# Where the halves of g lie in a partition: 0 and 192 bytes modulo 256, in place of 192 and 192

## The chip, the cores and the metric

The kernel runs on one NeuronCore of a Trainium2 chip. The metric is the device time of one execution in microseconds: 608.89 us, the median of 3 runs (608.73 to 609.63). The engines are named as in the profile: PE is TensorE's matmuls and PEld its weight loads, DVE is VectorE, ACT ScalarE, POOL GpSimd and SP SyncE, which issues the transfers.

## The reference

A windowed attention with block summaries, then a feed-forward layer with a squared ReLU:

```python
k_sum = k.reshape(B, H, nb, block, D).max(axis=3)
v_sum = v.reshape(B, H, nb, block, D).mean(axis=3)
scores_l = scale * q @ k.T          # masked to |i - j| < 16
scores_s = scale * q @ k_sum.T + np.log(block)
a = softmax(concatenate([scores_l, scores_s], -1))
x = a @ concatenate([v, v_sum], axis=2)      # heads put side by side: 3072 x 512
h = x @ w_in                                 # 512 x 2048
r = np.maximum(h, 0.0)
g = s * (r * r) + b
return g @ w_out                             # 2048 x 512
```

There are 4 batches of 768 rows, 8 heads of 64, blocks of 32 keys. All inputs are float32.

## The kernel before

The 3072 rows are worked in 12 chunks of 256 (three to a batch). For each chunk the attention of its four pairs of heads gives x in transposed form; then the hidden layer is made in 16 blocks f of 128 features, and each block is projected back onto 512 output columns.

The feed-forward products keep float32's accuracy by splitting each operand into an upper half, rounded to the matmul's number format, and a lower half, the remainder: xh and xl, wh and wl, gh and gl. A product is the sum of three matmuls, lower x upper, upper x lower, upper x upper. For the hidden layer (`hidden`, L460) the weights are the stationary operand, which a weight load brings into TensorE before the matmul, and x streams past them, 256 columns at a time: per block 4 matmuls of xh with wl, 4 of xl with wh, 4 of xh with wh. For the projection (`project`, L504; the last four blocks in `project_last`, L514) g is the stationary operand and w_out's half streams past it, 512 columns at a time: per block and per 128 rows one matmul with gl and wh, one with gh and wl, one with gh and wh. So gh is loaded twice and gl once.

Two blocks share one tile of g, 128 x 512. It is made by `activate` (ScalarE: ReLU out of the accumulators at L468, square at L474), `scaled` (GpSimd, L481), `upper_rows` (VectorE, a cast into gh, L219) and `lower_rows` (VectorE, r minus gh into gl, L492). r has two buffers, gh and gl four each.

The order of work on every engine is written out: a long list of names for the first chunks, then a table of steps. From the third chunk on TensorE alternates between runs of 48 hidden matmuls (4 blocks) and runs of 24 projection matmuls (4 blocks of the earlier ones), and once in a chunk does the attention's value products (L417) and scores (L301) for later chunks.

The sums of v over blocks, for batches 1 to 3, are made on the way. For each of two groups g of heads `v_sum` reduces three thirds of v (VectorE, L172) into the tile vhalf, and `v_mean` scales it (ScalarE, L178) into vmean, from which four transfers take it to vsum. vhalf has two buffers, so that the second group can be reduced while the first still waits for its scaling.

Tiles lie in a partition one after the other, in the order in which their pools first see them. What matters here, as addresses in bytes within a partition, before the change:

| tile | buffers | address of each | modulo 256 |
|---|---|---|---|
| wh (w_in and w_out upper) | 8 | 4352 to 61696, 8192 apart | 0 |
| wl | 17, in a ring | 69888 to 135424, 4096 apart | 0 |
| xh, xl | 2 and 2 | 171456, 175552; 179648, 183744 | 192 |
| r | 2 | 187840, 189888 | 192 |
| gh | 4 | 191936, 193984, 196032, 198080 | 192 |
| gl | 4 | 200128, 202176, 204224, 206272 | 192 |
| vhalf | 2 | 208320, 208576 | 192 |

The parts of these tiles that a matmul or a load reads begin at multiples of 512 bytes from the tile's start, so they lie at the same place modulo 256 as the tile.

Of the kernel before, what the change touches and what calls it, by code (L numbers as in the profile page):

```python
# [11 lines left out]
F32 = mybir.dt.float32  # L12
# [7 lines left out]
P = 128  # L20
B, H, S, D = 4, 8, 768, 64
# [8 lines left out]
T = NSUB * SUB  # L30
# [14 lines left out]
def windowed_attention_then_relu2_ffn(ctx, tc, qk, vwin, kt, vt, kq, vrow, wp, out):  # L45
# [8 lines left out]
    p2 = ctx.enter_context(tc.tile_pool(name="p2", bufs=2))  # L54
# [48 lines left out]
    w_raw, w_f, w_h, w_l, held = {}, {}, {}, {}, {}  # L103
# [43 lines left out]
    kraw, ksum, vraw, vhalf, vsum = {}, {}, {}, {}, {}  # L147
# [19 lines left out]

    def v_sum(bi, g, third):
        if third == 0:
            vhalf[bi, g] = p2.tile([96, D], F32, name="vhalf")  # L170
        dst = vhalf[bi, g][:, slice(*THIRDS[third])]
        nc.vector.tensor_reduce(dst, vraw.pop((bi, g, third))[:96], axis=AX.X, op=ALU.add)  # L172

# [55 lines left out]
    def place(c):  # L229
        return c // PER_B, c % PER_B  # L230
# [205 lines left out]
    ph_of, gg, po = {}, {}, {}  # L436
# [25 lines left out]
            )  # L462

    def activate(c, q, other=0):
        gg[c, q] = r = p2.tile([P, 2 * T], F32, name="r")
        ph = ph_of.pop((c, q))
        if other < 2:
            nc.scalar.activation(r, ph, AF.Relu)  # L468
        else:
            nc.vector.tensor_scalar(r, ph, 0.0, None, ALU.max)  # L470
        if other % 2:
            nc.vector.tensor_tensor(r, r, r, ALU.mult)
        else:
            nc.scalar.activation(r, r, AF.Square)  # L474
# [13 lines left out]

    def lower_rows(c, q):
        g, gh = gg[c, q]  # L490
        gl = p2.tile([P, 2 * T], F32R, name="gl", bufs=4)
        nc.vector.tensor_tensor(gl, g, gh.bitcast(F32), ALU.subtract)  # L492
        gg[c, q] = gh, gl
# [68 lines left out]
    def of(fn, *more):  # L562
# [9 lines left out]
        "Ai": of(scale_weights, "in"), "Ao": of(scale_weights, "out"), "A": of(scale_weights, "both"),  # L572
        "Bi": of(convert_weights, "in"), "Bo": of(convert_weights, "out"), "D": of(convert_weights, "both"),
        "Y": hidden_part, "H": hidden, "J": activate, "G": scaled, "a": upper_rows, "b": lower_rows,
        "P": project, "O": evict, "h": upper_weights, "l": lower_weights,
    }
# [20 lines left out]
    for c in range(2, NC):  # L597
        bi, ci = place(c)
        for p in range(NPAIR):
# [4 lines left out]
            if ci == 0:  # L604
                then(base - 12 + p, LOAD, load_k, bi, p)
                then(base - 7 + p, ATT, k_max, bi, p)
                if p < 2:
                    for third in range(3):
                        then(base + v_at - 5 + third, LOAD, load_v, bi, p, third)
                        then(base + v_at - 2 + third // 2, ATT, v_sum, bi, p, third)  # L610
                    then(base + v_at, ATT, v_mean, bi, p)
# [23 lines left out]
    for i in range(NF, NC * NF):  # L635
        c, f = divmod(i, NF)

        then(i - i % 4, HID, hidden, c, f)
        if f % 2:
            for stage_of in (activate, scaled, upper_rows, lower_rows):  # L640
                then(i, CHAIN, stage_of, c, f // 2)
        if i >= NC * NF - 4:
            if f == NF - 1:
                then((i + 4) | 3, PROJ, project_last)
            continue
        then((i + 4) | 3, PROJ, project, c, f)
        if f == NF - 1:
            for t in range(T // P):
                then((i + 4) | 3, EVICT, evict, c, t)
# [60 lines left out]
```

## Time and profile before

| what | before |
|---|---|
| median of 3 runs | 608.89 us |
| the profiled execution, its time | 609.05 us |
| the profiled execution, its span | 607.3 us |
| granted TensorE clock | 0.999 |
| PE busy | 598.1 us (98%) |
| DVE, ACT, POOL busy | 419.5, 275.9, 138.9 us |
| L504, three groups of 376 matmuls | 148.0, 147.7, 147.5 us |
| L460, three groups of 760 matmuls | 119.0, 117.8, 117.6 us |

The span runs from the first to the last instruction; the time has some 1.75 us more around it. Matmuls overlap in the trace, since each is shown from its start to the end of its pipeline: the pace is read from the distance between starts, not from their lengths. In the chain of waits, "in order of time", a row gives start, length and what, with a run of one line's matmuls put together; the length of such a run is free of that overlap.

### The profile page before, as it was taken

Reading aid. Unit: us, or ns where it says so; the run is one execution under the profiler, and the core shown is the slowest. Engines: PE = TensorE matmul, PEld = TensorE weight load, DVE = VectorE, ACT = ScalarE, POOL = GpSimd, SP = SyncE. Lnnn points to the kernel's source line nnn. Section 1 sums busy time; section 2 is a strip of 40 time slices with the busy share of each in tenths; the row PEclk is TensorE's granted clock in tenths of the full one; section 3 lists DMA queues with packets and bytes.
Section 4 is the critical chain, followed back from the end, with each engine's and each line's share of the span. In section 5 each row is a group of like instructions: output and inputs, shape, how many; then the busy total and the mean of one; then the engine's idle time right before and its main releaser. Section 6 shows DMA issues by size and latency. Waiting matters only on the chain.

```text
span 607.3 us, 13540 instructions
## 1 busy us (share of the span) xinstructions
PE 598.1 (98%) x5240; PEld 539.7 (89%) x5240; DVE 419.5 (69%) x1128; ACT 275.9 (45%) x712; POOL 138.9 (23%) x275
## 2 busy tenths in 40 slices
PE   7999999999999999999999999999999999999997
PEld 6798898899989998998999899999998998899896
DVE  6999988789589378668758648847858827832212
ACT  5999998261352262263163254235235235223221
POOL 5420012211511411412141411331151151141110
PEclk9999999999999999999999999999999999999999
DMA  8999723025405016103503211600630500200000
GB/s 337 389 386 389 270 84 113 1 72 156 137 3 186 1 46 225 58 20 107 169 20 100 88 45 64 220 18 20 176 101 1 187 9 12 87 2 1 36 2 35
DMA packets 27281, 66.41 MB, mean 109 GB/s; under 512 B 3856, under 2 KB 4368, under 8 KB 27216
## 3 DMA queue, kind: packets, MB, share of 16 engines
q1 hardware_dynamic: 27216, 65.55, 31.0%
q8 instruction: 41, 0.67, 0.5%
q14 instruction: 24, 0.20, 0.1%
HBM read 59.09 MB, written 6.29 MB: 108 GB/s over the span
## 4 chain that ended last, share of the span: by engine, by line
PE 94%; ACT 3%; DMA 1%; DVE 1%; issue 0%; SPq 0%; DVEq 0%
PE ph L460 43%; PE po L504 43%; PE pav L417 4%; PE ps L301 3%; ACT pr L336 1%; DMA wraw<-in_wp_dram 1%; PE po L514 1%; PE pt L379 0%; PE ph L441 0%; ACT wraw L122 0%; ACT wraw L123 0%; SPq L240 0%; ACT pT L221 0%; DVE pr L346 0%; ACT vsum L221 0%
## 5 line engine op out<-in xcount | busy, mean ns | idle before, releaser
L481 POOL TENSOR_SCALAR r<-r,sb_col 128x512 f32<-128x512 f32 x85 | 69.4, 817 | 392.6 <-ACT r L474 259.6
L468 ACT ACTIVATE r<-ph 128x512 f32<-128x512 f32 x93 | 55.4, 596 | 206.8 <-PE ph L460 172.6
L504 PE MATMUL po<-wh,gh 128*128 128x512 f32 x376 | 148.0, 393 | 0.0
L504 PE MATMUL po<-wh,gl 128*128 128x512 f32 x376 | 147.7, 393 | 0.0
L504 PE MATMUL po<-wl,gh 128*128 128x512 f32 x376 | 147.5, 392 | 0.0
L219 DVE CAST gh<-r 128x512 fp32r<-128x512 f32 x88 | 38.1, 433 | 131.7 <-POOL r L481 130.8
L368 DVE STREAM_TRANSPOSE pT<-pr 32x256 f32<-32x256 f32 x288 | 125.4, 436 | 4.1
L460 PE MATMUL ph<-xh,wl 128*128 128x256 f32 x760 | 119.0, 279 | 0.0
L460 PE MATMUL ph<-xl,wh 128*128 128x256 f32 x760 | 117.8, 277 | 0.0
L460 PE MATMUL ph<-xh,wh 128*128 128x256 f32 x760 | 117.6, 277 | 0.0
L460 PEld LDWEIGHTS ph<-xh,wl 128*128 128x128 f32 x760 | 104.8, 188 | 5.2 <-DVE wl L144 0.3
L460 PEld LDWEIGHTS ph<-xl,wh 128*128 128x128 f32 x760 | 101.3, 188 | 0.0
L460 PEld LDWEIGHTS ph<-xh,wh 128*128 128x128 f32 x760 | 100.7, 188 | 0.0
L504 PEld LDWEIGHTS po<-wh,gl 128*128 128x128 f32 x376 | 70.6, 188 | 15.0 <-issue 1.1
L504 PEld LDWEIGHTS po<-wh,gh 128*128 128x128 f32 x376 | 70.7, 188 | 14.4
L504 PEld LDWEIGHTS po<-wl,gh 128*128 128x128 f32 x376 | 70.6, 188 | 13.8
L336 ACT ACTIVATE pr<-pr,mn 128x120 f32<-128x120 f32 x176 | 67.0, 383 | 22.2 <-DVE mn L323 22.0
L492 DVE TENSOR_TENSOR gl<-r,gh 128x512 fp32r<-128x512 f32 x96 | 69.3, 722 | 4.1 <-ACT gh L221 1.3
L474 ACT ACTIVATE r<-r 128x512 f32<-128x512 f32 x92 | 58.2, 632 | 5.7 <-DVE r L470 2.9
L263 POOL COPY vw<-vsum 24x256 f32<-24x256 f32 x88 | 47.2, 574 | 26.5 <-DMA vsum<-vmean 13.2
L346 DVE TENSOR_TENSOR pr<-pr,rs 128x480 f32<-128x480 f32 x48 | 32.9, 685 | 2.4 <-ACT pr L336 0.5
L221 ACT COPY o<-po 128x512 f32<-128x512 f32 (+1 forms) x23 | 13.1, 570 | 46.3 <-PE po L504 36.0
(94 smaller groups left out, 495.3 us busy)
## 6 DMA issues: line engine op xcount, KB each, us to landing
wraw<-in_wp_dram SPq DMA_DIRECT2D x32, 512.0 KB, 8.3
qk<-in_qk_dram SPq DMA_DIRECT2D x44, 369.0 KB, 5.7
vw<-in_vwin_dram SPq DMA_DIRECT2D x48, 256.0 KB, 3.6
out_dram<-o SPq DMA_DIRECT2D x22, 256.0 KB, 2.0
kraw<-in_kt_dram SPq DMA_DIRECT2D x12, 384.0 KB, 5.5
vraw<-in_vt_dram SPq DMA_DIRECT2D x12, 252.0 KB, 3.1
kq<-in_kq_dram SPq DMA_DIRECT2D x4, 512.0 KB
vraw<-in_vt_dram SPq DMA_DIRECT2D x6, 264.0 KB, 3.2
```

The costliest lines, as they stand in the source:

```text
L219: nc.vector.tensor_copy(out_, in_)
L263: nc.gpsimd.tensor_copy(vw_t[c, p][WIN:KR, e], vsum[bi][WIN : WIN + NB, 2 * p + e, :].unsqueeze(1).to_broadcast([NB, NSUB, D]),)
L336: nc.scalar.activation(pr, pr, AF.Exp, bias=mn_of[c, p][:, n : n + 1], scale=-1.0, accum_out=sm_of[c, p][:, n : n + 1])
L346: nc.vector.tensor_tensor(pr, pr, rs.unsqueeze(2).to_broadcast([P, 4, KR]), ALU.mult)
L368: nc.vector.transpose(to[BLOCK * k : BLOCK * (k + 1), :, rows], src)
L417: nc.tensor.matmul(oi, vw[:KR, e, i, :], pi[:KR], start=True, stop=True)
L460: nc.tensor.matmul(ph, w[:, kc * P : (kc + 1) * P], x[:, kc], start=(n == 0), stop=(n == len(terms) - 1))
L468: nc.scalar.activation(r, ph, AF.Relu)
L474: nc.scalar.activation(r, r, AF.Square)
L481: (nc.vector if other else nc.gpsimd).tensor_scalar(g, g, s_col, b_col, ALU.mult, ALU.add)
L492: nc.vector.tensor_tensor(gl, g, gh.bitcast(F32), ALU.subtract)
L504: nc.tensor.matmul(po[c, t], a[:, t * P : (t + 1) * P], w[:, 512:], start=(f == 0 and n == 0), stop=(f == NF - 1 and n == len(terms) - 1),)
```

## The change

The upper halves gh are put at 0 bytes modulo 256; everything that lies behind gl stays where it was. The two buffers of r are made 32 bytes longer each, which moves gh by 64 bytes; a tile of 192 bytes, which nothing writes or reads, is placed between gh and gl; and vhalf, which lies behind gl, has one buffer in place of two, which gives the 256 bytes back.

```diff
     def v_sum(bi, g, third):
         if third == 0:
-            vhalf[bi, g] = p2.tile([96, D], F32, name="vhalf")
+            vhalf[bi, g] = p2.tile([96, D], F32, name="vhalf", bufs=1)
         dst = vhalf[bi, g][:, slice(*THIRDS[third])]
         nc.vector.tensor_reduce(dst, vraw.pop((bi, g, third))[:96], axis=AX.X, op=ALU.add)
...
     def activate(c, q, other=0):
-        gg[c, q] = r = p2.tile([P, 2 * T], F32, name="r")
+        gg[c, q] = r = p2.tile([P, 2 * T + 8], F32, name="r")[:, : 2 * T]
         ph = ph_of.pop((c, q))
...
     def lower_rows(c, q):
         g, gh = gg[c, q]
+        if ("gap", 0) not in held:
+            held["gap", 0] = p2.tile([P, 48], F32, name="gap", bufs=1)
         gl = p2.tile([P, 2 * T], F32R, name="gl", bufs=4)
```

| tile | address of each, changed kernel | modulo 256 |
|---|---|---|
| r | 187840, 189920 | 192, 224 |
| gh | 192000, 194048, 196096, 198144 | 0 |
| gl | 200384, 202432, 204480, 206528 | 192 |
| vhalf | 208576 | 192 |

All other tiles keep their addresses. The order of instructions is the same on every engine. One wait is added, three times (once for each of batches 1 to 3): on VectorE, at the first reduction of the second group of heads (`vhalf` is the tile of sums, `vraw` the raw v). Before:

```order
L172 TENSOR_REDUCE vhalf<-vraw 96x21 [waits DMAHW4_49]
L172 TENSOR_REDUCE vhalf<-vraw 96x22 [waits DMAHW2_49]
L172 TENSOR_REDUCE vhalf<-vraw 96x21 [waits DMAHW5_49]
L368 STREAM_TRANSPOSE pT<-pr 32x8x32 x4
L219 CAST gh<-r 128x512 [waits PE_49,Pool_49]
L492 TENSOR_TENSOR gl<-r,gh 128x512 [waits DVE_49]
```

The same place in the changed kernel, whose later line numbers are two higher:

```order
L172 TENSOR_REDUCE vhalf<-vraw 96x21 [waits DMAHW4_49]
L172 TENSOR_REDUCE vhalf<-vraw 96x22 [waits DMAHW2_49,Activation_49]
L172 TENSOR_REDUCE vhalf<-vraw 96x21 [waits DMAHW5_49]
L368 STREAM_TRANSPOSE pT<-pr 32x8x32 x4
L219 CAST gh<-r 128x512 [waits PE_49,Pool_49]
L494 TENSOR_TENSOR gl<-r,gh 128x512 [waits DVE_49]
```

The reduction of 22 columns, the first of the second group, now waits for ScalarE too: for the scaling of the first group's sums (L178), which reads the buffer that it is to overwrite.

## The prediction

> **What bounds the kernel now.** I read the page's busy shares and chain first, then the chain in order of time for the steady part, then the order of single matmuls there. First the page:
>
> ```profile
> span 607.3 us, 13540 instructions
> PE 598.1 (98%) x5240; PEld 539.7 (89%) x5240; DVE 419.5 (69%) x1128; ACT 275.9 (45%) x712; POOL 138.9 (23%) x275
> ...
> PEclk9999999999999999999999999999999999999999
> ...
> PE 94%; ACT 3%; DMA 1%; DVE 1%; issue 0%; SPq 0%; DVEq 0%
> ...
> L460 PE MATMUL ph<-xh,wl 128*128 128x256 f32 x760 | 119.0, 279 | 0.0
> ```
>
> TensorE is busy 98% of the span at a full granted clock and holds 94% of the chain. Nothing that another engine does can win much; what counts is the pace at which TensorE starts one matmul after the other. The chain in order of time (start, length, what) shows that pace for one chunk of 256 rows:
>
> ```profile
> 311.19 5.70 PE po L504 x24
> 316.89 5.47 PE ph L460 x48
> 322.36 5.49 PE po L504 x24
> 327.85 5.47 PE ph L460 x48
> 333.32 5.49 PE po L504 x24
> ...
> 355.24 2.02 PE pav L417 x64
> 357.25 1.80 PE ps L301 x64
> 359.05 5.70 PE po L504 x24
> ```
>
> A chunk takes 359.05 - 311.19 = 47.9 us, and all but the 2.02 and 1.80 of them, 44.0, are runs of hidden (L460) and project (L504). The same two runs look different earlier:
>
> ```profile
> 124.63 5.66 PE ph L460 x48
> 130.29 5.51 PE po L504 x24
> 135.80 5.66 PE ph L460 x48
> ...
> 158.14 5.65 PE ph L460 x48
> 163.79 2.02 PE pav L417 x64
> ...
> 173.31 5.47 PE ph L460 x48
> ```
>
> Here 48 matmuls of the same shape take 5.66 us, after the next attention stage 5.47 us. Inside a run, the single matmuls (start, length, instruction):
>
> ```profile
> 326.31 0.39 PE L504 MATMUL po<-wh,gl 128*128 128x512 f32 x1
> 326.54 0.39 PE L504 MATMUL po<-wl,gh 128*128 128x512 f32 x1
> 326.77 0.39 PE L504 MATMUL po<-wh,gh 128*128 128x512 f32 x1
> 327.00 0.39 PE L504 MATMUL po<-wh,gl 128*128 128x512 f32 x1
> ...
> 327.69 0.64 PE L460 MATMUL ph<-xh,wl 128*128 128x256 f32 x4
> 328.16 0.62 PE L460 MATMUL ph<-xl,wh 128*128 128x256 f32 x4
> 328.62 0.62 PE L460 MATMUL ph<-xh,wh 128*128 128x256 f32 x4
> 329.07 0.62 PE L460 MATMUL ph<-xh,wl 128*128 128x256 f32 x4
> 329.53 0.62 PE L460 MATMUL ph<-xl,wh 128*128 128x256 f32 x4
> ```
>
> Settled hidden matmuls start 4 in 0.453 us (328.62 to 329.53 is 0.91 us for 8), 113.3 ns each for 256 columns. Two of these, 226.7 ns, is the measure for a projection of 512 columns: 24 of them would take 5.44 us, and the 48 hidden ones 5.44 us too. Against it there are three excesses: (a) a projection run takes 5.49, 0.05 us over; (b) a hidden run takes 5.47, 0.03 over, and the rows show where: the first four after a projection need 0.47 us, not 0.453; (c) the runs of 5.66 us, 0.22 over, of which four stand between 124 and 164 us.
>
> **The change part by part.** No instruction is added, removed or moved.
>
> *Places.* gh goes from byte 192 to byte 0 of a 256-byte stretch; gl, xh, xl stay at 192 and the weights at 0; r's second buffer goes from 192 to 224. Two of every three weight loads in a projection read gh. Whether a place costs time is nowhere seen by itself in this trace, so I bound it. What speaks for a cost is that the two kinds of run differ in just this: hidden loads its stationary operand from 0 and streams from 192, and settles without excess; project loads from 192 and streams from 0, and never settles: 0.05 us over in every run. Each load overlaps the matmul before it:
>
> ```profile
> L504 PEld LDWEIGHTS po<-wh,gl x376: 186/188/190, 42.2 to 597.2; 128*128 128x128 f32 x188
> L504 PE MATMUL po<-wh,gl x376: 388/388/505, 42.3 to 597.4; 128*128 128x512 f32 x188
> L504 PE MATMUL po<-wl,gh x376: 388/392/398, 42.5 to 597.6; 128*128 128x512 f32 x188
> L504 PE MATMUL po<-wh,gh x376: 388/394/398, 42.7 to 597.9; 128*128 128x512 f32 x188
> ```
>
> A load of 188 ns runs while the matmul before it streams, and the three kinds differ (388, 392, 394 ns) at equal places, so the two streams of reads seem to get into each other's way, in a rhythm of three. Upper bound of the gain: all three excesses go. (a) 1128 matmuls are 47 runs of 24, 47 x 0.05 = 2.4 us; (b) 2280 hidden ones are 47 runs of 48, 47 x 0.03 = 1.4 us; (c) four runs at 5.66 instead of 5.47, 0.8 us. Together 4.6. Lower bound: the hidden runs of the nine settled chunks, four in each, fall to 5.66: 36 x 0.19 = 6.8 us lost. I take the value nearest to the settled row: gh loaded from 0 behaves as the hidden loads from 0 do, gl stays as it is. That is two thirds of (a), 1.6 us. Of (b), which is what a projection run leaves behind for the next four or five matmuls, I take half, 0.7, since the last load of a run changes and the hidden loads do not. Of (c) nothing. Sum: -2.3 us.
>
> *One buffer for the half sums.* The first reduction of the second group now waits until ScalarE has read the first group's sums. VectorE and ScalarE there:
>
> ```profile
> 146.91 2.40 DVE L172 TENSOR_REDUCE vhalf<-vraw 96x21 f32<-96x672 f32 x3
> 149.34 1.78 DVE L368 STREAM_TRANSPOSE pT<-pr 32x256 f32<-32x256 f32 x4
> ```
>
> ```profile
> 147.79 0.26 ACT L178 ACTIVATE vmean<-vhalf 96x64 f32<-96x64 f32 x1 [4.99 <-DVE vhalf L172]
> ```
>
> ScalarE stands idle 4.99 us for that very reduction and ends at 148.05. The second of the three reductions would start at about 147.7 (0.8 us after the first) and now starts about 0.4 us later, three times in the kernel: 1.2 us of VectorE. Behind it in VectorE's order stand one more reduction, four transposes, and the next gh and gl. Of what L504 waits for, over the whole kernel, these rows name VectorE (us, times):
>
> ```profile
>   DVE gh L219: 0.2, 1
>   DVE gl L492: 0.2, 1
> ```
>
> That is 0.4 us; gh and gl have four buffers each, and VectorE is idle 31% of the time. I cost it at nothing on the path, 1.2 us if that cover were gone. The raw tiles of v come free 0.4 us later, and with them SyncE's next loads; DMA is 1% of the chain.
>
> *VectorE, ScalarE and GpSimd on the moved tiles.* Should the subtraction of L492 take 0.1 us more or less in each of 96 calls, VectorE's 419.5 us change by 9.6, off the path: nothing.
>
> Sum: 609.05 (the profiled execution, span 607.3 and 1.75 around it) - 2.3 = 606.75; the median of the runs shown is 608.89, 0.16 lower, so **606.6 us**.
>
> **The rivals.** *Places don't matter.* The rhythm of three arises at equal places, and the 5.66 and 5.47 us runs have the same instructions at the same addresses. So the excess may come from how loads and matmuls are queued, and the moved bytes do nothing: 47 runs of 5.49 stay 5.49, the wait is covered, **608.9 us**. Against it: that the run which never settles is the one with the other places.
>
> The Trainium skill has a rule that makes this rival: "SBUF — State Buffer", section "Who interferes with whom", gives TensorE two independent read ports, one for the moving operand and one for weight loads, and says that only the port pair shared by VectorE and GpSimd causes contention. By that rule the sum would be 0 and the time 608.9. The excess of 0.05 us in every projection run does not decide it, since the rule leaves room for a cause outside the memory.
>
> *The other rhythm takes hold (slower).* Rows (c) show a second stable pace of the hidden matmuls, 5.66 / 48 = 118 ns, that lasts from the projection before it until the attention stage (L417, L301) breaks it at 164 us. Which pace holds is set by how the run of projections ends, and that is what the change alters in each run. If gh at 0 under weights at 0 leaves the streams in the bad phase, all 36 settled hidden runs go to 5.66: +6.8, **615.7 us**; if it does so in half of them, +3.4, 612.3. It decides from the first projection run after 167 us that is followed by 5.66. For it: four runs in a row did this, with 5.51 in the projections between. Against it: since 173 us no run did. A milder form is one more stall of the size of (a) in each run, +2.4, 611.3.
>
> *Everything settles.* All of (a), (b), (c) goes: -4.6, **604.3 us**. I count it as the far end of the forecast.
>
> **How the numbers follow.** The forecast, gh's loads stop costing, with its own range of 604.0 to 607.7: 0.45. Places don't matter: 0.28. The other rhythm or a further stall: 0.27. A measurement of this kernel tells 0.2%, 1.2 us, from no change, so faster means below 607.7 and slower above 610.1; the three cases fall on the three sides, and give 0.45, 0.28 and 0.27. For the range I go down to 603.9, a little below the far end for excesses of early runs that I did not count, and up to 612.0, which takes in the milder form and up to half of the runs in the bad pace; about 0.07 is left out below and 0.1 above.
>
> **What would show it.** Forecast right: L504 x24 in the chain at 5.45 to 5.47 in place of 5.49, L460 x48 at 5.44 to 5.47. No coupling: both rows the same to 0.01 us and the three matmul lengths still 388, 392, 394. The bad rhythm: L460 x48 at 5.66 after 170 us. The wait on the half sums: a gap of about 0.4 us on VectorE before L172, three times, and no new row of TensorE waiting for VectorE. I would be wrong from the ground up if the time moved by more than 5 us down (then the measure of 113.3 ns for 256 columns itself depends on places), or if the change of time stood in L417, L301 or a wait and not in the two paces.

## The result, and the profile after

The changed kernel takes 612.56 us, the median of 8 runs (611.54 to 614.0), against 609.46 us for the kernel before in the same measurement (8 runs, 608.73 to 611.5). The ratio is 1.005, with a 95% interval of 1.004 to 1.006: half a per cent slower, where 606.6 us had been forecast. The profiled execution took 612.33 us with a span of 610.6, 3.3 us more than before.

The page of the changed kernel:

```profile
span 610.6 us, 13543 instructions
...
PE 601.1 (98%) x5240; PEld 540.4 (89%) x5240; DVE 418.7 (69%) x1128; ACT 276.4 (45%) x712; POOL 135.9 (22%) x275
...
PEclk9999999999999999999999999999999999999999
...
L506 PE MATMUL po<-wh,gl 128*128 128x512 f32 x376 | 150.1, 399 | 0.0
...
L460 PE MATMUL ph<-xh,wl 128*128 128x256 f32 x760 | 118.8, 278 | 0.0
```

TensorE is as busy as before, at the same clock, with the same number of matmuls: it does the same work at a slower pace. The chain of waits in order of time (start, length, what) for the chunk that was shown of before:

```profile
312.21 5.75 PE po L506 x24
317.96 5.66 PE ph L460 x48
323.61 5.55 PE po L506 x24
329.17 5.45 PE ph L460 x48
334.62 5.54 PE po L506 x24
340.16 5.47 PE ph L460 x48
...
356.64 2.02 PE pav L417 x64
358.66 1.80 PE ps L301 x64
360.46 5.75 PE po L506 x24
```

A chunk takes 360.46 - 312.21 = 48.25 us, before 359.05 - 311.19 = 47.86. Two rows carry it. A run of 24 projections is 5.54 or 5.55, not 5.49. And the first hidden run of the chunk is 5.66, not 5.47; the other three are as they were, or 0.02 shorter. The first run of 5.66 after the attention stage at 165 us is this one, where the kernel before had 5.47:

```profile
167.47 5.75 PE po L506 x24
173.22 5.66 PE ph L460 x48
```

The two kernels issue the same matmuls in the same order, so each stretch of one line's matmuls in one trace has its counterpart in the other. From 165 us on, the 37 projection runs of 24 cost 1.98 us more, eight first hidden runs 1.50 us more, the other 28 hidden runs 0.13 less. Before 165 us hidden runs cost 1.22 less (four of 48 fall from 5.66 to 5.47 and one from 5.78 to 5.53, 1.00 together), projections 0.34 more, value products (L417) and the earliest hidden products (L441) 0.81 more. With 0.05 for the last projections and small pieces of other lines the sum is 3.4 us on TensorE.

How one projection matmul changes is seen in the answer by line for L506 (lengths in ns, least/median/greatest):

```profile
L506 PE MATMUL po<-wh,gl x376: 389/392/505, 42.2 to 600.6; 128*128 128x512 f32 x188
...
L506 PE MATMUL po<-wl,gh x376: 387/389/402, 42.5 to 600.8; 128*128 128x512 f32 x188
...
L506 PE MATMUL po<-wh,gh x376: 388/394/398, 42.7 to 601.1; 128*128 128x512 f32 x188
```

The medians were 388, 392, 394. That the first rose and the second fell speaks for an effect of the places, but a length is not the pace, and a median hides the loss: the mean of the first is 399 ns on the page, 393 before. The distances between starts show it. In the 31 runs of 24 that follow hidden matmuls, the matmul after the one with wh and gl starts 233.7 ns later on the mean, before 226.5; after the one with wl and gh it is 229.4, as before; after the one with wh and gh 230.4, before 231.3. The whole loss stands in the first of the three distances.

The one buffer for the half sums shows as the diff said. VectorE in the changed kernel (start, length, what, and in brackets the idle time ahead of it with its releaser):

```profile
147.31 0.85 DVE L172 TENSOR_REDUCE vhalf<-vraw 96x21 f32<-96x672 f32 x1
148.48 1.64 DVE L172 TENSOR_REDUCE vhalf<-vraw 96x22 f32<-96x704 f32 x2 [0.33 <-ACT vmean L178]
```

VectorE waits 0.33 us for the scaling. At the next value products TensorE now waits:

```profile
163.03 0.80 PE L417 MATMUL pav<-pT,vw 120*64 120x64 f32 x18
164.06 1.61 PE L417 MATMUL pav<-pT,vw 120*64 120x64 f32 x46 [0.23 <-POOL vw L263]
```

In the kernel before, the same 64 ran without a gap:

```profile
163.72 2.09 PE L417 MATMUL pav<-pT,vw 120*64 120x64 f32 x64
```

Now they begin 0.7 us earlier, because the hidden runs ahead of them got faster, the four rows of 5.66 among them. GpSimd's copy of the sums (L263) is not ready, and 0.55 us of the gain is given back there.

### The profile page after: what moved, and what is told of

It reads as the page before. It is cut to its first block, busy times and chain, and to the rows that moved or that the text cites. A ratio compares the mean times of both kernels' runs of the same rounds, so it can differ in the third digit from the quotient of the medians.

```text
span 610.6 us, 13543 instructions
## 1 busy us (share of the span) xinstructions
PE 601.1 (98%) x5240; PEld 540.4 (89%) x5240; DVE 418.7 (69%) x1128; ACT 276.4 (45%) x712; POOL 135.9 (22%) x275
## 4 chain that ended last, share of the span: by engine, by line
PE 88%; DVE 5%; ACT 4%; DMA 1%; issue 1%; POOL 1%; SPq 0%; POOLq 0%; DVEq 0%; ACTq 0%
PE po L506 40%; PE ph L460 39%; PE pav L417 4%; PE ps L301 3%; ACT pr L336 2%; DVE pT L368 2%; PE po L516 1%; DMA vsum<-vmean 1%; DVE pr L346 1%; DMA kq<-in_kq_dram 1%; DVE vhalf L172 1%; POOL vw L263 1%; DVE gl L494 1%; PE pt L379 0%; PE ph L441 0%
## 5 line engine op out<-in xcount | busy, mean ns | idle before, releaser
L506 PE MATMUL po<-wh,gl 128*128 128x512 f32 x376 | 150.1, 399 | 0.0
L506 PE MATMUL po<-wh,gh 128*128 128x512 f32 x376 | 148.0, 394 | 0.0
L506 PE MATMUL po<-wl,gh 128*128 128x512 f32 x376 | 147.0, 391 | 0.0
L460 PE MATMUL ph<-xh,wl 128*128 128x256 f32 x760 | 118.8, 278 | 0.0
L460 PE MATMUL ph<-xl,wh 128*128 128x256 f32 x760 | 117.9, 277 | 0.0
L460 PE MATMUL ph<-xh,wh 128*128 128x256 f32 x760 | 117.8, 277 | 0.0
L460 PEld LDWEIGHTS ph<-xh,wl 128*128 128x128 f32 x760 | 105.0, 188 | 4.9 <-DVE wl L144 0.2
L460 PEld LDWEIGHTS ph<-xl,wh 128*128 128x128 f32 x760 | 101.2, 188 | 0.0
L460 PEld LDWEIGHTS ph<-xh,wh 128*128 128x128 f32 x760 | 100.9, 188 | 0.0
L506 PEld LDWEIGHTS po<-wh,gh 128*128 128x128 f32 x376 | 70.5, 188 | 16.8
L506 PEld LDWEIGHTS po<-wh,gl 128*128 128x128 f32 x376 | 70.5, 188 | 15.1 <-issue 1.3
L506 PEld LDWEIGHTS po<-wl,gh 128*128 128x128 f32 x376 | 70.8, 188 | 13.6
L263 POOL COPY vw<-vsum 24x256 f32<-24x256 f32 x88 | 45.5, 554 | 25.0 <-issue 8.9
```

The source lines that it names most:

```text
L263: nc.gpsimd.tensor_copy(vw_t[c, p][WIN:KR, e], vsum[bi][WIN : WIN + NB, 2 * p + e, :].unsqueeze(1).to_broadcast([NB, NSUB, D]),)
L460: nc.tensor.matmul(ph, w[:, kc * P : (kc + 1) * P], x[:, kc], start=(n == 0), stop=(n == len(terms) - 1))
L506: nc.tensor.matmul(po[c, t], a[:, t * P : (t + 1) * P], w[:, 512:], start=(f == 0 and n == 0), stop=(f == NF - 1 and n == len(terms) - 1),)
```

## The experiments

Apart from the one buffer, and but for the two kernels with a step, all kernels differ from the kernel before only in where tiles lie. A gap is a tile that nobody uses, its second number counts words of 4 bytes, and it moves what is first seen after it: xh, xl, r, gh, gl, vhalf stand in that order. Unless said otherwise there is one buffer for vhalf, as in the change, and everything behind gl keeps its address; in the five kernels with x or xl moved and g at 0, r moves too and the tiles behind vhalf lie 64 bytes further. After the first edit the line of vhalf is left out of the cuts shown, and mostly the line `if ... not in held:` ahead of a gap, which makes that tile only once. The weights lie at 0 modulo 256. All distances of places here are modulo 256.

Each run has a time, with the median of before in the same measurement, a ratio with its 95% interval, and two paces read from the chain in order of time and from the starts of the matmuls in ns. The measure is 226.7 ns for a projection and 113.3 ns for a hidden matmul. A hidden run is called settled when its matmuls come to start 113.3 ns apart, and slow when they stay at 117.8 or more. One execution of each kernel was traced, so counts of hidden runs at either pace are those of one execution. The theories, which the expectations name by letters or numbers, ask whether the place of a tile counts, or its distance from the operand that streams against it, or something that the projection run leaves behind for the hidden run. To begin with they were: places count; or the one buffer counts; or only the rhythm does.

**One buffer alone.** The places stay.

```diff
-            vhalf[bi, g] = p2.tile([96, D], F32, name="vhalf")
+            vhalf[bi, g] = p2.tile([96, D], F32, name="vhalf", bufs=1)
...
         gl = p2.tile([P, 2 * T], F32R, name="gl", bufs=4)
+            held["gap", 2] = p2.tile([P, 64], F32, name="gap2", bufs=1)
```

> The one buffer for half sums alone: gh and gl stay at 192, an unused tile of 256 bytes behind gl keeps all other addresses. Theory P (the places of gh and gl set the pace): the projection runs return to 5.49 us for 24 matmuls, the hidden runs to 5.47, and only the wait of the value products at 164 us can remain; 609.0 to 609.6. Rival V (the wait on the half sums makes the loss, directly or by what it leaves behind): 611 to 612.6, projection runs at 5.55.

Measured 609.39 against 609.27 us, ratio 1.0003 (0.9991 to 1.0016). The wait costs nothing that can be told: on TensorE L417 grew by 0.19 us. (In other kernels here L417 and the scores, L301, together grew by up to 1.9 us; so much of a time below can stand there and not in the two paces.) This kernel's chain has something else, at a place where the kernel before had 5.47:

```profile
316.44 5.65 PE ph L460 x48
322.10 5.51 PE po L506 x24
327.61 5.66 PE ph L460 x48
333.26 5.51 PE po L506 x24
```

One whole chunk, with the old places, is in the slow hidden pace; the chunks around it are not. So the slow pace is not tied to a place of gh and gl alone, nor to the early part of the kernel.

**Both halves at 64.**

```diff
+            held["gap", 0] = p2.tile([P, 32], F32, name="gap0", bufs=1)
         gh = p2.tile([P, 2 * T], F32R, name="gh", bufs=4)
...
         gl = p2.tile([P, 2 * T], F32R, name="gl", bufs=4)
+            held["gap", 2] = p2.tile([P, 32], F32, name="gap2", bufs=1)
```

> gh and gl both at 64 modulo 256, where the weights stream from 0: the same distance from streamed to loaded operand, +64, as in the hidden runs. Theory R (the distance modulo 256 between the streamed operand and the operand being loaded sets the pace): the projection settles as hidden does, 24 matmuls in 5.44 to 5.46, 606 to 607. Rival A (only an operand loaded from 0 modulo 256 settles): 64 is no better than 192, 609. Rival B (the pace only depends on how a run is entered): any time from 606 to 616, with 5.66 in hidden runs.

Measured 617.09 us, ratio 1.0127 (1.0113 to 1.0141). Projections cost 4.7 us more, hidden 3.4 more. In the chain:

```profile
320.48 5.46 PE ph L460 x48
325.94 5.59 PE po L508 x24
331.53 5.66 PE ph L460 x48
337.19 5.60 PE po L508 x24
342.79 5.46 PE ph L460 x48
```

The projections start 231 and 236 ns apart in turn, 233.3 on the mean, and the hidden runs alternate between the two paces within one chunk. Theory R falls in this form: 64 is the distance at which the hidden loads stand, and the projections do not settle at it. The time lies outside what all three theories expected.

**Both halves at 0.** What the forecast had assumed for gh, done for both.

```diff
+            held["gap", 0] = p2.tile([P, 16], F32, name="gap0", bufs=1)
         gh = p2.tile([P, 2 * T], F32R, name="gh", bufs=4)
...
         gl = p2.tile([P, 2 * T], F32R, name="gl", bufs=4)
+            held["gap", 2] = p2.tile([P, 48], F32, name="gap2", bufs=1)
```

> gh and gl both at 0, no mix of places. Theory R: distance 0 is worse than 192 by what the change shows for two of three loads (0.05 us a run of 24), so 5.57 a run and 47 x 0.08 = 3.8 us over before, about 613. Rival M (it is the mix of 0 and 192 that costs): a rhythm of its own with one place, 5.49 or less, 609 or below. Rival A (loads from 0 settle): 5.44, 606 to 607.

Measured 613.76 us, ratio 1.0081 (1.0069 to 1.0094):

```profile
324.92 5.44 PE po L508 x24
330.36 5.65 PE ph L460 x48
```

The projections have no excess left, 24 in 5.44 us: 1.9 us less in all, where the prediction's bound for (a) was 2.4. But every hidden run is now at 117.8 ns, 7.1 us more. Rival A had the projections right; no theory had the hidden runs. Theory R's 613 came out, but not by its way, a run of 24 in 5.57. Both the forecast's gain and the rival of the other rhythm are in this one picture.

**Everything 64 bytes further, weights included.** Two buffers for vhalf.

```diff
+    const.tile([P, 16], F32, name="ahead")
     mean4 = const.tile([P, 2 * NB - 4], F32, name="mean4")
```

> The kernel before with 64 unused bytes ahead of the weights: all tiles behind, weights, x, r, gh and gl, move by 64, so gh and gl come to 0 and the weights to 64, and every distance stays. Theory R: nothing changes, 24 projections in 5.49, 609.0 to 609.8. Rival A (the place itself counts): gh and gl from 0 give another pace, by what the both-at-0 run gives, and the hidden runs, whose weights are then loaded from 64, lose their 5.47.

Measured 609.67 us, ratio 1.0007 (0.9998 to 1.0016):

```profile
323.63 5.49 PE po L505 x24
329.12 5.47 PE ph L461 x48
```

Weights, x and g all changed place and the paces did not. So, for this one shift, it is the distance between the tiles that counts, not where one of them lies.

**Is the hidden pace one of distance as well?** First x and g together at 0 (two buffers for vhalf), then x alone.

```diff
+                held["xgap"] = p2.tile([P, 16], F32, name="xgap", bufs=1)
             xt[c] = p2.tile([P, NKC, T], F32R, name="xh", tag="xh")
```

> One unused tile of 64 bytes ahead of xh brings xh, xl, gh and gl to 0 modulo 256 like the weights; vhalf has two buffers as before. Theory R, now with the signs of the first runs (a matmul whose loaded operand lies at the same place modulo 256 as its streamed one has no excess): projections 5.44 for 24 as with both halves of g at 0, and hidden runs 5.44 for 48 in place of 5.65, so 604 to 605, faster than before. Rival H (hidden runs go to the slow rhythm of 118 ns whenever the projection before them leaves without excess, wherever x lies): projections 5.44 but hidden 5.65, 613 to 614.

Measured 619.58 us against 608.81, ratio 1.0175 (1.0161 to 1.0189): hidden matmuls at 120 ns, 11.7 us more; projections 1.1 us less:

```profile
332.40 5.75 PE ph L462 x48
338.15 5.47 PE po L506 x24
```

Neither theory had this: one expected 5.44 for the hidden runs, the other 5.65.

```diff
+                held["xgap"] = p2.tile([P, 16], F32, name="xgap", bufs=1)
             xt[c] = p2.tile([P, NKC, T], F32R, name="xh", tag="xh")
...
+            held["gap", 0] = p2.tile([P, 48], F32, name="gap0", bufs=1)
         gh = p2.tile([P, 2 * T], F32R, name="gh", bufs=4)
```

> xh and xl at 0, gh and gl left at 192 (and r at 0). Theory R: hidden runs lose what they have (5.47 to 5.44 or a little over, and no run of 5.65), projections stay at 5.49: 606.5 to 608. Rival H: hidden runs keep 5.47 with the slow ones among them, 609.

Measured 621.04 us, ratio 1.02 (1.0186 to 1.0214), the slowest of all:

```profile
322.34 5.76 PE ph L462 x48
328.10 5.50 PE po L508 x24
333.60 5.75 PE ph L462 x48
```

The projections are untouched at 229 ns, the hidden runs are at 120 ns in every run. Both expectations missed (606.5 to 608, and 609). Distance 0, which is best for the projections, gives the slowest hidden matmuls seen. To put everything at one place does not serve both.

**Both halves at 128.**

```diff
+            held["gap", 0] = p2.tile([P, 48], F32, name="gap0", bufs=1)
         gh = p2.tile([P, 2 * T], F32R, name="gh", bufs=4)
...
         gl = p2.tile([P, 2 * T], F32R, name="gl", bufs=4)
+            held["gap", 2] = p2.tile([P, 16], F32, name="gap2", bufs=1)
```

> gh and gl both at 128, distance 128, the fourth place. Measured so far per projection matmul over 226.7 ns: distance 0 none, 64 some 6.7 ns, 192 some 2.2 ns. Theory R says nothing of where between these 128 lies: between 192 and 64 if the cost falls steadily with the distance, 4.4 ns, so 24 in 5.55, 611 to 618 with the hidden runs in either rhythm.

Measured 611.71 us, ratio 1.0048 (1.0036 to 1.0061):

```profile
324.01 5.58 PE po L508 x24
329.59 5.45 PE ph L460 x48
335.04 5.58 PE po L508 x24
```

The mirror of both at 0: projections slower, at 232.3 ns (3.9 us more; 5.58 for 24 where 5.55 was expected), and all hidden runs but one at 113.3 ns (1.5 us less).

**The change with the halves exchanged: gh at 192, gl at 0.**

```diff
         g, gh = gg[c, q]
+            held["gap", 1] = p2.tile([P, 16], F32, name="gap1", bufs=1)
         gl = p2.tile([P, 2 * T], F32R, name="gl", bufs=4)
+            held["gap", 2] = p2.tile([P, 48], F32, name="gap2", bufs=1)
```

> gh at 192 and gl at 0, the change the other way round. Theory X (a change of place from one load to the next costs, on top of the places): two changes of place in every three loads as in the change itself, so 24 projections in 5.53 to 5.56 although two loads lie as before. Rival S (each load has the price of its own distance, the prices add): one load of three at no excess, two as before, so less than before, 5.47 to 5.48 for 24.

Measured 615.62 us, ratio 1.0112 (1.0096 to 1.0127):

```profile
330.09 5.65 PE ph L460 x48
335.75 5.49 PE po L508 x24
341.24 5.65 PE ph L460 x48
```

One third of the loads at 0 gains nothing on the projections (5.49 as before), and 40 of 41 hidden runs are slow. Both at 0 gives 5.44, both at 192 gives 5.49, two thirds at 0 (the change) 5.55: a mixture is not between its parts. Theory X and rival S both miss: the exchange costs neither 5.53 to 5.56 nor 5.47 to 5.48.

**x at 64 and at 128, g at 0.**

```diff
+                held["xgap"] = p2.tile([P, 32], F32, name="xgap", bufs=1)
             xt[c] = p2.tile([P, NKC, T], F32R, name="xh", tag="xh")
...
+            held["gap", 0] = p2.tile([P, 48], F32, name="gap0", bufs=1)
         gh = p2.tile([P, 2 * T], F32R, name="gh", bufs=4)
```

> xh and xl at 64, so the hidden weights at 0 are loaded at distance 192; gh and gl both at 0, which gave projections without excess. Theory R has the hidden runs so far: distance 64 gives 113 or 118 ns, 0 gives 120. If distance 192 stands to 64 as in the projection (2.2 against 6.7 ns), hidden settles at 113 to 115, 5.44 to 5.52 for 48, projections 5.44, so 604 to 608, faster than before. Rival H (after a projection without excess hidden is slow whatever the place): 5.65 or more, 613 and up.

Measured 615.43 us against 609.53, ratio 1.0096 (1.0081 to 1.0111): hidden 117.8 ns, as Rival H had it, projections 226.7 ns after some seven matmuls at 224 to 241 ns at the start of a run.

```diff
+                held["xgap"] = p2.tile([P, 48], F32, name="xgap", bufs=1)
             xt[c] = p2.tile([P, NKC, T], F32R, name="xh", tag="xh")
...
+            held["gap", 0] = p2.tile([P, 32], F32, name="gap0", bufs=1)
         gh = p2.tile([P, 2 * T], F32R, name="gh", bufs=4)
```

> xh and xl at 128, the fourth place, hidden loads at distance 128; gh and gl both at 0. Theory R: projections 5.44 again (the third kernel with g at 0), hidden between the paces of distance 64 and 192, 5.44 to 5.75, so 604 to 618. Rival H: hidden 5.65 or more, 613 and up.

Measured 620.36 us, ratio 1.0176 (1.0161 to 1.0191):

```profile
321.57 5.76 PE ph L462 x48
327.33 5.48 PE po L508 x24
```

Hidden matmuls are at 120 ns, as with x at 0, which again only Rival H allows.

**Loads of every second row of g.** Loads with a step of 8 bytes take even rows, then odd rows, of a block, and the results are stored accordingly; once with g at 128, once at 0. This asked whether the load's own way through the 256 bytes sets the paces, in which case less than the measure could be reached.

```diff
-                    po[c, t], a[:, t * P : (t + 1) * P], w[:, 512:],
+                    po[c, t], a[:, t : T : 2], w[:, 512:],
...
+            held["gap", 0] = p2.tile([P, 48], F32, name="gap0", bufs=1)
         gh = p2.tile([P, 2 * T], F32R, name="gh", bufs=4)
```

> The projection loads every second row of g (even rows of a chunk for one output tile, odd for the other; the stores put them back in order), so a load of 128 values reaches over 1024 bytes in place of 512; gh and gl at 128. Theory L (four places of 64 bytes in every 256; a stream of 9 bytes a ns laps a load of half that speed about twice, and each meeting costs 6.7 ns, which is what the 226.7 ns of a projection hold beyond 213.3): at equal speed and two places apart the two never meet, 24 projections in 5.12 to 5.25 in place of 5.49, and the kernel in 590 to 600. Rival F (226.7 and 113.3 ns are the pace of these matmuls by themselves, meetings only add): 5.44 at best, 606 and up. Rival W (a load with a step takes longer by itself): slower than 612.

Measured 615.92 us, ratio 1.0103 (1.0088 to 1.0118): 5.55 to 5.57 for 24, hidden runs half slow (20 of 41).

```diff
-                    po[c, t], a[:, t * P : (t + 1) * P], w[:, 512:],
+                    po[c, t], a[:, t : T : 2], w[:, 512:],
...
+            held["gap", 0] = p2.tile([P, 16], F32, name="gap0", bufs=1)
         gh = p2.tile([P, 2 * T], F32R, name="gh", bufs=4)
```

> The same loads of every second row with gh and gl at 0, so load and stream begin in one place. Theory L: at equal speed they meet once at the start and then keep apart, so 24 projections in 5.12 to 5.3, little or nothing worse than at 128. Rival F: 5.44 at best. Rival W: slower than 612.

Measured 611.81 us, ratio 1.0051 (1.0034 to 1.0068):

```profile
328.15 5.45 PE ph L460 x48
333.60 5.59 PE po L508 x24
```

Distance 0 with a step is at 233.3 ns, without it at 226.7: the load's first address alone does not settle the pace. The loads with a step also last longer, 193 ns at 0 and 196 at 128, against 188 without; whether their pattern or their length counts was not separated. The theory that less than the measure can be had falls: no settled pace here is below 226.7 and 113.3 ns, and no run shows the 213.3 ns that it started from. Rival F holds in both kernels, Rival W's times (slower than 612) in the first.

**Is it a matter of steps of 64 bytes?** Both halves at 32, then at 224.

```diff
+            held["gap", 0] = p2.tile([P, 24], F32, name="gap0", bufs=1)
         gh = p2.tile([P, 2 * T], F32R, name="gh", bufs=4)
...
         gl = p2.tile([P, 2 * T], F32R, name="gl", bufs=4)
+            held["gap", 2] = p2.tile([P, 40], F32, name="gap2", bufs=1)
```

> gh and gl both at 32, between 0 (226.7 ns a projection matmul) and 64 (233.3). Theory S (places count in steps of 64 bytes, and 32 begins in the step of 0): a pace of 226.7 to 228, 24 in 5.44 to 5.47; the hidden runs then 5.65 as with g at 0, 613. Theory T (the pace changes in finer steps): between, 5.5 to 5.55 for 24, and the hidden runs can fall either way, 604 to 616.

Measured 612.62 us against 609.95, ratio 1.0051 (1.0033 to 1.0068):

```profile
330.49 5.46 PE ph L460 x48
335.94 5.59 PE po L508 x24
```

```diff
+            held["gap", 0] = p2.tile([P, 8], F32, name="gap0", bufs=1)
         gh = p2.tile([P, 2 * T], F32R, name="gh", bufs=4)
...
         gl = p2.tile([P, 2 * T], F32R, name="gl", bufs=4)
+            held["gap", 2] = p2.tile([P, 56], F32, name="gap2", bufs=1)
```

> gh and gl both at 224, between 192 (228.9 ns) and 0 (226.7). Theory S: as at 192, 24 in 5.49, hidden 5.47, 609. Theory T: between the two, 5.45 to 5.48; if the projection then leaves as at 192, hidden stays at 5.47 and the kernel comes to 607 to 608, else 613.

Measured 618.6 us, ratio 1.0145 (1.0128 to 1.0163). Both have projections at 233.3 ns, the first with settled hidden runs (39 of 41), the second with 31 of 41 at 117.8 ns. Neither 32 does as 0, nor 224 as 192: two places within one step of 64 bytes do not give the same pace. Nor do 32 and 224 lie between their neighbours, as Theory T had it.

**Two more places of x, with g at 0:** both halves of x at 224 (two buffers for vhalf), and xh at 192 with xl at 128.

```diff
+                held["xgap"] = p2.tile([P, 8], F32, name="xgap", bufs=1)
             xt[c] = p2.tile([P, NKC, T], F32R, name="xh", tag="xh")
...
+            held["gap", 0] = p2.tile([P, 8], F32, name="gap0", bufs=1)
         gh = p2.tile([P, 2 * T], F32R, name="gh", bufs=4)
```

> gh and gl at 0 as in the run without excess in the projection, xh and xl at 224 in place of 192, so the hidden loads stand 32 bytes off the streamed operand in place of 64. Theory H (after a projection without excess the hidden run always starts in the slow rhythm, and the place of x only sets how slow it is): 5.65 or more for 48, 613 and up. Rival K (whether the hidden run settles depends on the place of x together with how it is entered): 5.44 to 5.47 for 48, 604 to 605, faster than before.

```diff
+                held["xlgap"] = p2.tile([P, 48], F32, name="xlgap", bufs=1)
             xl[c] = p2.tile([P, NKC, T], F32R, name="xl", tag="xl")
...
+            held["gap", 0] = p2.tile([P, 32], F32, name="gap0", bufs=1)
         gh = p2.tile([P, 2 * T], F32R, name="gh", bufs=4)
```

> gh and gl at 0, xh at 192 and xl at 128: the four matmuls with xl in every twelve get another place, so the rhythm of the hidden run is disturbed every twelve matmuls. Theory H: slow, 118 ns or more, 613 and up. Rival K: a disturbance lets it fall into the settled pace of 113.3 ns for at least the eight matmuls with xh, 5.45 to 5.55 for 48, 604 to 609. Theory X (changes of place cost by themselves, as gh and gl apart did): over 5.66, 614 and up.

Measured 616.91 us, ratio 1.012 (1.0103 to 1.0137), and 615.14 us, ratio 1.0095 (1.0075 to 1.0115). Hidden runs take 5.68 in the first and 5.67 in the second: no place of x was found that keeps the hidden runs settled while g lies at 0 and is loaded without a step, as Theory H had it.

**Half and half, in both orders.** In every run of 24 the tiles of two of its four blocks lie at 0, those of the other two at 192. If what the run leaves behind comes from its last place, the two orders differ.

```diff
+            held["gap", q % 2] = p2.tile([P, (64, 192)[q % 2] // 4], F32, name=f"gap{q % 2}", bufs=1)
-        gh = p2.tile([P, 2 * T], F32R, name="gh", bufs=4)
+        gh = p2.tile([P, 2 * T], F32R, name="gh", tag=f"gh{q % 2}", bufs=2)
...
-        gl = p2.tile([P, 2 * T], F32R, name="gl", bufs=4)
+        gl = p2.tile([P, 2 * T], F32R, name="gl", tag=f"gl{q % 2}", bufs=2)
```

> g at 0 in the first two of the four blocks of every run of projections (the even tiles of g), at 192 as before in the other two. Theory 1, pace by distance within the run and the rhythm of the hidden run by how the projections leave it: the first twelve projections at 226.7 ns, the last twelve at 229, 24 in 5.46 to 5.47; the run ends from 192 as in the kernel before, so 48 hidden in 5.47 after 170 us: 1.0 to 1.4 us less than before, 607.6 to 608.1 against 608.9 to 609.3. Theory 2, every change of place disturbs: going from 0 to 192 within a run gives the pace of the mixed tiles (231 ns), 24 in 5.53 or more, and part of the hidden runs at 5.66: 611 to 613.

```diff
+        if q == 1 and ("gap", 0) not in held:
+            held["gap", 0] = p2.tile([P, 16], F32, name="gap0", bufs=1)
-        gh = p2.tile([P, 2 * T], F32R, name="gh", bufs=4)
+        gh = p2.tile([P, 2 * T], F32R, name="gh", tag=f"gh{q % 2}", bufs=2)
...
-        gl = p2.tile([P, 2 * T], F32R, name="gl", bufs=4)
+        gl = p2.tile([P, 2 * T], F32R, name="gl", tag=f"gl{q % 2}", bufs=2)
```

> The mirror: the first two blocks of every run at 192, the last two at 0. Theory 1: projections as in the other order, 24 in 5.46 to 5.47, but the run ends without excess from 0, as in the kernel with both halves at 0, and 48 hidden need 5.65 in all chunks: projections 1.2 us less, hidden 6 to 7 us more, 613.5 to 615. Theory 2 (the exit does not decide, only a change of place disturbs): same as the other order to 0.5 us.

Measured 616.24 us against 609.61, ratio 1.0106 (1.0091 to 1.0122), and 617.76 us, ratio 1.013 (1.0114 to 1.0145). The first order:

```profile
326.49 5.47 PE po L506 x24
331.95 5.65 PE ph L460 x48
```

The second:

```profile
327.05 5.49 PE po L508 x24
332.53 5.66 PE ph L460 x48
```

Within a run the pace follows the place, once the run is under way, where nothing is mixed in one block: in the first order 226.7 ns for twelve, then the rhythm of 226, 229, 232, and 5.47, as Theory 1 had it; in the second five matmuls at 231 to 237, the rhythm up to the twelfth, then 226.7. The first order also bears on the 256 bytes themselves. Its tiles at 192 lie at 192 modulo 512, those of the kernel before at 448, and the rhythm is the same. But the hidden run is slow after both orders, which no theory had for the first. The last place does not decide; nor does a change of place within the run as such, since both at 0 has none and is slow too.

**What goes with the pace.** These are the distances in ns between the starts of successive matmuls: the last nine of a projection run, the last of these up to the first hidden matmul, and then the first hidden ones. The time is that of the first hidden start.

```
before, 135.6 us        229 232 226 229 232 226 229 231 227 | 118 117 118 118 117 119 117 118   slow
before, 338.6 us        226 229 232 226 229 232 226 229 231 | 117 117 117 123 118 113 114 113   settles
changed, 317.8 us       241 237 232 231 224 232 226 227 227 | 117 118 118 117 118 118 118 117   slow
changed, 329.0 us       226 227 226 236 228 233 241 238 233 | 120 116 114 113 114 113 113 114   settles
both at 0, 341.3 us     227 226 227 227 226 227 227 226 227 | 117 118 118 118 117 119 117 118   slow
0 then 192, 342.9 us    229 232 225 230 232 225 230 231 227 | 117 118 118 118 117 119 117 118   slow
both at 128, 340.4 us   232 228 230 233 241 232 231 232 233 | 120 116 114 113 114 113 113 114   settles
```

The first two rows are one kernel, with the same tiles at the same addresses. The rhythm is the same, turned by one step: the short distance stands after the matmul with wh and gh in the slow row, after the one with wh and gl in the other. Where the run ends on its short step, 227, the hidden matmuls stay at 117.8 ns; where it ends on 231, the fourth hidden one takes a further 123, and they settle at 113.3. Since 24 is a multiple of three, the rhythm returns to the same step at the end of every run. The row "0 then 192", the first order of half and half, has the old rhythm in its end, turned as in the slow row.

Over the kernel before, the changed kernel and all the kernels with xh and xl both at 192 from the weights, 14 in all with 41 hidden runs of 48 each, the last distance and the pace go together so:

```
                        settles   slow
last distance <= 228          0    201
last distance >= 229        313     60
```

Of the 60 exceptions 51 belong to both at 64 and both at 224, where no distance in the settled rhythm is below 229; there, with two exceptions, the runs that end on 229 to 231 are slow and those that end on 233 or more settle. The other nine stand ahead of 137 us, one or two in a kernel. Where x, or xl alone, lies at 0, 64, 128 or 224, all hidden runs are slow whatever the last distance.

This is a regularity in 574 runs, found after the fact and not tested by an edit that turns the rhythm alone. The last distance ends at the first hidden start, so it may be the first sign of a pace and not its cause. What in the hardware carries it is open.

## Why the prediction was wrong

**What bounds the kernel** held. The 3.3 us stand in the two paces, all but about 0.8 us, which stands in L417 and L441. The measure of 226.7 and 113.3 ns also held: both were reached as settled paces, and neither was undercut in any kernel here.

**Term (a), -1.6 us: this is the step that failed.** The prediction put it as "gh loaded from 0 behaves as the hidden loads from 0 do, gl stays as it is". Measured is +2.3 us on L506. The reason given, that the places of load and stream set the excess, was right: with both halves at 0 the excess is gone, 5.44 us. What failed is the two thirds. The effects of gh and gl do not add up load by load. A load begins with the matmul ahead of it (in the kernel before the load of gh at 326.32 us, the matmul with wh and gl at 326.31). So two distances have a load of gh in them, the ones after wh, gl and after wl, gh. These should have come down, and the first rose by 7.2 ns while the second stayed. With gh and gl at two distances the steady three-step rhythm of 226, 229, 232 is replaced by an uneven one that goes up to 241 (both halves at 128 show 241 too, so a mixture is not the only way to it). The exchange of the halves shows the same from the other side: there the distance after wh, gh, which holds the load from 0, fell from 231.3 to 229.1 ns, the other two rose by about 1.1 each, and nothing was gained. Why the change's mixture costs more than either place is open.

The prediction also read the lengths 388, 392, 394 as three kinds of matmul. They go with the steps of the rhythm, which in one and the same kernel stands turned against the operands, as the first two rows of the distances show.

The Trainium skill, in "SBUF — State Buffer", section "Who interferes with whom", says that only the port pair of VectorE and GpSimd causes contention and that TensorE never waits on anyone. By that rule all of these kernels would have kept the paces of the kernel before, 5.49 and 5.47. The traces do not agree for this pattern: 24 projections took 5.44, 5.49, 5.58 and 5.59 us at distances 0, 192, 128 and 32, with the instructions in the same order. Whether it is a port, a bank or a queue that is shared cannot be told from the runs.

**Terms (b) and (c), -0.7 and 0.** The hidden runs that settle gained 0.13 us over 28 runs, not 0.7 over all. And (c) did not stand still. The runs of 5.66 between 124 and 164 us fell to 5.47 (with one other run 1.00 us less), and eight others, the first of each chunk from 173 us on except the last chunk, rose to 5.66 (1.50 more). The table above fits both but for one run: the last distance of the projection run ahead of those eight is 226 or 227 in the trace of the changed kernel, and that of all runs ahead of a settled one 230 or more. Of the four early runs of the kernel before three ended on 226 or 227; the first, at 124.5 us, ended on 233 and was slow all the same. The prediction put (c) at nothing without giving a reason, and took the rows of 5.66 for something that belongs to a stretch of the kernel. In the traces they go with the step on which a rhythm ends.

**The one buffer, 0 us** was right within what can be told: 609.39 against 609.27 us alone. The bound of 1.2 us was also a fair one, though the place was wrong. The prediction looked for a late gh or gl; VectorE waits 0.33 us as it said (0.4), but TensorE then waits at L417 for the sums themselves, through the transfers to vsum and GpSimd's copy. In the change this took 0.55 us. TensorE arrived there 0.7 us earlier; how much of the wait the buffer adds was not separated.

**The rivals.** The one of "the other rhythm" was nearest: it named the place (the end of a projection run), the size (0.19 us for a run) and the first sign (a 5.66 after 167 us, which came at 173.22 us). It gave 612.3 for half of the 36 runs; eight were slow, and its milder form, one more stall of the size of (a) in each run, was there too: +2.4 by the prediction, +2.3 measured. Each of them alone was priced; that both come together, less what the early runs give back, makes the 612.56. That 612.3 lies so near is luck, since it came from 18 hidden runs at 5.66 and no further stall; so is the +2.4, whose size was taken over from (a) without a reason of its own. The evidence held against this rival, that no run since 173 us was slow, was weak: those 36 runs were not 36 separate trials. A rhythm that returns to the same step after every 24 repeats its outcome, so it was nearer to one trial for each attention stage, after which the rhythm starts anew: the changed kernel's rows of 5.66 are the first hidden run after such a stage in eight of nine chunks.

"Places don't matter" is excluded by both halves at 0 and at 64, 613.76 and 617.09 us with the same order of instructions. Its observation, that the same instructions at the same addresses run at two paces, was right nonetheless: one kernel has both paces, and by the table the end of the projection run goes with which one follows. "Everything settles" is not excluded as a number. Both at 0 had 7.06 us more in L460 than the kernel before; were its hidden runs as settled as before, it would take 613.76 - 7.1 = 606.7 us, an estimate. No version reached that, and none beat the kernel before. Turning the rhythm by one step ahead of the hidden run, by another order of the three terms or by a run of 23 or 25, is the edit that would test this; it was not tried.

## What to carry to other kernels

Where weight loads and matmuls follow one another without a gap, as here, the distance modulo 256 bytes between the operand that is loaded and the one that streams can be a parameter of the pace. In this kernel it was worth up to 3% in a run of projections and 6% in a hidden run; it is to be measured for all operands of a run together, since a part moved alone can cost more than either place. The pace of a run can also go with how the run ahead of it ends: read the chain in order of time for both, and the last distances of the one ahead. A stable row in one profile of such a kernel is weak evidence that it stays so: count how often the rhythm was started anew, not how often it was repeated.

## What was not expected of the hardware

Projection matmuls of 512 columns, each with one load of 128 columns, came to these mean distances by the place of g (both halves; weights at 0, x at 192; the row of 192 is the kernel before):

| g modulo 256 | 24 projections | ns for one | 48 hidden after it |
|---|---|---|---|
| 0 | 5.44 us | 226.7 | 5.65 us in all |
| 32 | 5.59 | 233.3 | 5.45 in 39 of 41 |
| 64 | 5.59 | 233.3 | 5.46 and 5.66, half each |
| 128 | 5.58 | 232.3 | 5.45 in 40 of 41 |
| 192 | 5.49 | 228.9 | 5.47 in 37 of 41 |
| 224 | 5.60 | 233.3 | 5.66 in 31 of 41 |
| 0, step of 8 bytes | 5.59 | 233.3 | 5.45 in 40 of 41 |

Hidden matmuls of 256 columns had two paces at one and the same place of x, 113.3 and 117.8 ns, each kept for a whole run of 48, and a third, 120 ns, with x at 0 or 128. The load that best suits the projection, from the same place as its stream, gives the hidden matmul its slowest pace. No settled pace here came below 226.7 ns for 512 columns. For a single matmul by itself the Trainium skill's formula in "TensorE: Matmul & The Clock Gate", section "Back-to-back issue gap", gives 512 / 2.4 + 2.5 = 215.8 ns, an estimate, which no run of this case shows.
